# Two heads of a pair on alternate partition rows, in a fused attention and mixture-of-experts kernel

## The chip, the cores and the metric

The kernel runs on one core of a Trainium2 chip. The metric is device time in microseconds of one execution. Before the change three runs took 537.25, 535.7 and 528.64 us, so the median is 535.7 us.

## The reference, cut to what matters

The input has a batch of 8, with 8 heads, 576 positions and 64 numbers per head. Two attentions are computed and added: one over queries, keys and values that are averaged over four neighbouring positions, its output repeated four times, and one local attention in which a position sees the positions less than four away. The sum, as 4608 tokens of 512 numbers, goes through a layer of 8 experts.

```python
q_d = q.reshape(B, H, Sd, factor, D).mean(axis=3)      # the same for k, v
out_up = np.repeat(sm_attn(q_d, k_d, v_d), factor, axis=2)
mask = np.abs(pos[:, None] - pos[None, :]) < factor
scores = np.where(mask, scale * np.matmul(q, k.transpose(0, 1, 3, 2)), -1000000000.0)
x = out_up + softmax(scores) @ v                       # as 4608 rows of 512
...
do_compute = x @ w_skip > 0
e_idx = argmax(x @ w_gate, axis=1)
y[mask] = gate_w[mask, None] * (np.maximum(x[mask] @ w1[e], 0.0) @ w2[e])
out = x + y                                            # x alone where a token is skipped
```

## The kernel before, in words

The program has two parts. The attention part works through 36 tiles of 128 tokens; a tile is four groups of 32 queries, and a batch has 18 groups, so four and a half tiles. It writes its rows x to HBM and sorts the tokens to the experts on the way (`route`). The expert part then gathers each expert's rows with indirect DMAs (`load_x`), multiplies (`up_mm` L829, `down_mm` L849) and scatters the results.

**Pairs of heads.** Two heads form a pair, and there are four pairs. The queries of a pair fill 128 partitions: `Q` is [128, 4 x 576], 64 partitions for each head of a pair. The keys lie in `KB`, [128, 2, KF]: the second index is the head of the pair, and in the half of the partitions that belongs to the other head there are zeros. One product of 128 rows thus gives the scores of both heads next to each other. Before the change a pair's first head has partitions 0 to 63, its second 64 to 127 (`halves`, L162). There are two key buffers, used by batches in turn, so the zeros are written once: those of the first buffer by DVE and POOL (L635), copied by ScalarE to the second (L667), and three zero columns at each end by DVE (L642). `KD` has the same layout for the keys summed over four positions.

**V windows.** A group of 32 queries sees 38 keys, padded to KR = 48. `VB` is [96, 2, 4, 4, 64], rows of head 0 in partitions 0 to 47 and of head 1 in 48 to 95, again with zeros in the other half; `load_v` (L190) brings a tile's windows with two DMAs of 48 rows. There are three such buffers. The tile of weights `Et` is [128, 8 heads, 48], so that a pair's 96 columns, transposed, meet the 96 rows of `VB`.

**Pooled branch of a batch.** `load_q`, `load_k` (two DMAs, one for each head of the pairs; batch 0 loads in three column pieces), `load_v4`; `pool_q`, `pool_k` (L232: for each pair two sums, one per head, over four positions, on DVE, for one pair of batch 0 on POOL), `d_scores` (L243, PE), `d_max`, `d_exp`, `d_transpose`, `d_values`, `d_out`, `d_hi` and `d_lo`. Its result `up` is spread to the tiles by a product.

**One tile.** `load_v`, `scores` (L347: mask, then 32 products), `s_max` (L360), `s_sub` (L364, out of PSUM into `Et`), `s_exp` (L369), `s_sum` (L372), `add_eps`, `recip`, `norm` (L382, on POOL), `p_transpose` (L386), `p_evac`, `up_mm` (L397, needs the batch's `up`), `values` (L411), `x_out` (L418), `store_x`, then the logits for the experts.

**Order of the work.** Every step is entered in a list `nodes`, and the numbers in `ORDER` say in which order the list is carried out (L763). Each engine takes its instructions in that order, SyncE's queue with the loads and stores too: a load that waits for its buffer holds those behind it. The expert part is written out in order and has no such list.

Of the kernel before, what the change touches and what calls it, by code (L numbers as in the profile page):

```python
# [109 lines left out]
)  # L110

@with_exitstack
def tile_attention_moe(ctx, tc, qT, kT, vW, v4, vr, mask, cst, ups, cid, w9, w1, w2, out):
    nc = tc.nc
# [520 lines left out]
    for c in range(3):  # L638
        node(load_q, 0, slice(c, c + 1))
        for hh in range(2):  # L640
            node(load_k, 0, hh, slice(c, c + 1))
# [395 lines left out]
```

## Time and profile before

| what | us |
|---|---|
| runs | 528.64, 535.7, 537.25 |
| profiled execution, its own time | 527.66 |
| its span, first to last instruction | 525.5 |
| PE busy in the span | 454.1 |
| DVE busy | 317.7 |
| ScalarE busy | 248.6 |
| POOL busy | 171.7 |

The mean granted clock of PE is 0.963. A profile row for a group of instructions has line, engine, operation, output<-inputs, shapes and count, then the busy time in us and the mean ns of one, then the idle time of the engine just before them and what ended it. A table of stretches has the busy time of each engine in each stretch, the granted clock, the share of the time in which the 16 DMA engines were busy, and what they moved in GB/s. A share over 1 means packets that overlap on an engine. `hh` and the like are names of tiles in the program; SPq is SyncE's queue, which issues the loads.

### The profile page before, as it was taken

What the parts mean: (1) busy time and instruction counts of PE and PEld (TensorE: products, weight loads), DVE (VectorE), ACT (ScalarE), POOL (GpSimd) and SP (SyncE); (2) the same over time, 40 slices, a digit from 0 to 9 for tenths busy, and PEclk for the clock granted to TensorE, in tenths of its full rate; (3) what the DMA queues carried; (4) which work ended last, traced back from release to release, by engine and by line L of the source; (5) the groups of instructions that cost most, each with busy time, mean ns of one, the idle gap of its engine ahead of it and who ended that gap; (6) DMA issues with size and microseconds to landing.
All of it is one profiled execution on the core that took longest, in us unless ns stands there. A gap on an engine that the chain in (4) does not pass through costs nothing. (4 is left out here: it accounts for less than half of the span.)

```text
span 525.5 us, 13816 instructions
## 1 busy us (share of the span) xinstructions
PE 454.1 (86%) x5642; PEld 385.5 (73%) x5642; DVE 317.7 (60%) x653; ACT 248.6 (47%) x562; POOL 171.7 (33%) x184
## 2 busy tenths in 40 slices
PE   0488887986979887999649999999999999999991
PEld 0356775874857765788539998999998989898981
DVE  4988747576496675843633564555667664667521
ACT  1655764942737455755233543434454633355310
POOL 9486727064361544311060031050314040010102
PEclk9999998997999998999958999999999999999997
DMA  8999898899875797244164346553566754455201
GB/s 235 305 253 261 253 251 229 256 245 284 208 229 168 204 273 200 71 147 127 48 218 157 122 166 223 161 183 127 179 229 223 248 190 173 162 191 187 83 4 54
DMA packets 33885, 98.89 MB, mean 188 GB/s; under 512 B 5101, under 2 KB 6381, under 8 KB 33794
## 3 DMA queue, kind: packets, MB, share of 16 engines
q1 hardware_dynamic: 29954, 86.52, 56.0%
q0 software_dynamic: 3840, 11.09, 5.8%
q8 instruction: 65, 1.06, 0.9%
q14 instruction: 26, 0.21, 0.1%
HBM read 83.36 MB, written 15.73 MB: 189 GB/s over the span
## 5 line engine op out<-in xcount | busy, mean ns | idle before, releaser
L798 POOL DMA_INDIRECT out<-Y,six x24 | 24.3, 1012 | 193.3 <-DVE Y L856 190.4
L829 PE MATMUL ph<-xth,w1h 128*128 128x384 f32 (+2 forms) x256 | 82.0, 320 | 0.7 <-ACT xth L820 0.7
L829 PE MATMUL ph<-xtl,w1h 128*128 128x384 f32 (+2 forms) x256 | 80.1, 313 | 0.1
L829 PE MATMUL ph<-xth,w1l 128*128 128x384 f32 (+2 forms) x256 | 80.0, 313 | 0.0
L849 PE MATMUL py<-w2h,hh 128*128 128x512 f32 x168 | 65.8, 392 | 0.4
L849 PE MATMUL py<-w2l,hh 128*128 128x512 f32 x168 | 65.8, 391 | 0.0
L849 PE MATMUL py<-w2h,hl 128*128 128x512 f32 x168 | 65.7, 391 | 0.0
L241 DVE TENSOR_REDUCE KD<-KB 64x144 f32<-64x576 f32 x62 | 46.1, 744 | 23.5 <-DMA KB<-kT 22.8
L838 ACT ACTIVATE hh<-ph 128x384 fp32r<-128x384 f32 x64 | 31.5, 492 | 58.8 <-PE ph L829 30.7
L839 DVE SCALAR_TENSOR_TENSOR hl<-ph,hh 128x384 fp32r<-128x384 f32 x64 | 34.7, 553 | 38.3 <-ACT hh L838 38.3
L829 PEld LDWEIGHTS ph<-xth,w1h 128*128 128x128 f32 x256 | 49.4, 193 | 1.5 <-ACT xth L820 1.1
L829 PEld LDWEIGHTS ph<-xtl,w1h 128*128 128x128 f32 x256 | 49.4, 193 | 0.8 <-issue 0.4
L829 PEld LDWEIGHTS ph<-xth,w1l 128*128 128x128 f32 x256 | 49.2, 192 | 0.0
L383 POOL TENSOR_TENSOR Et<-Et,r 128x304 f32<-128x304 f32 x36 | 26.5, 740 | 60.6 <-DVE r L380 36.8
L594 DVE TENSOR_TENSOR w2l<-raw,w2h 128x1024 fp32r<-128x1024 f32 x32 | 39.0, 1220 | 10.7 <-ACT w2h L593 10.5
L609 DVE TENSOR_TENSOR w1l<-raw,w1h 128x1024 fp32r<-128x1024 f32 x32 | 39.5, 1233 | 7.3 <-ACT w1h L604 7.3
L415 PE MATMUL O<-VB,PT 96*32 96x128 f32 x1152 | 39.0, 276 | 5.3 <-ACT PT L394 3.0
L820 ACT CAST xth<-Tx 128x512 fp32r<-128x512 f32 x22 | 12.9, 588 | 63.2 <-PE Tx L817 57.3
L593 ACT CAST w2h<-raw 128x1024 fp32r<-128x1024 f32 x32 | 33.6, 1049 | 14.4 <-PE py L849 14.4
L821 DVE TENSOR_TENSOR xtl<-Tx,xth 128x512 fp32r<-128x512 f32 x22 | 15.2, 692 | 40.8 <-ACT xth L820 40.2
L357 PE MATMUL S<-KB,Q 128*32 128x76 f32 x1152 | 29.3, 244 | 11.3 <-DVE KB L623 10.5
L415 PEld LDWEIGHTS O<-VB,PT 96*32 96x32 f32 x1152 | 30.6, 110 | 11.1 <-issue 6.1
(141 smaller groups left out, 959.3 us busy)
## 6 DMA issues: line engine op xcount, KB each, us to landing
raw<-w SPq DMA_DIRECT2D x64, 512.0 KB, 4.6
VB<-vW SPq DMA_DIRECT2D x72, 192.0 KB, 5.0
out<-X SPq DMA_DIRECT2D x36, 256.0 KB, 5.1
V<-v SPq DMA_DIRECT2D x16, 512.0 KB, 7.6
KB<-kT SPq DMA_DIRECT2D x14, 576.0 KB, 10.3
Q<-qT SPq DMA_DIRECT2D x7, 1152.0 KB, 9.0
Q<-qT SPq DMA_DIRECT2D x3, 384.0 KB, 3.1
KB<-kT SPq DMA_DIRECT2D x6, 192.0 KB, 5.4
```

Source lines behind the costliest of these rows:

```text
L241: nc.vector.tensor_reduce(out=kd, in_=kv, axis=AX.X, op=ALU.add)
L357: nc.tensor.matmul(Sv[quad[j], 2 * p:2 * p + 2], lhsT=B[b]["Q"][:, o:o + QG], rhs=KBs[b % 2][:, :, k:k + KW], start=False, stop=p == 3)
L383: nc.gpsimd.tensor_tensor(out=TT[i]["E"], in0=TT[i]["E"], in1=TT[i]["r"][:, :, None].to_broadcast([128, H, KW]), op=ALU.mult)
L415: nc.tensor.matmul(O[quad[j], 128 * a:128 * a + 128], lhsT=PT[:, a, quad[j]], rhs=VB[:, :, a, j, :], start=False, stop=a == 3)
L593: nc.scalar.copy(out=hf, in_=raw)
L594: nc.vector.tensor_tensor(out=flat(lo), in0=raw, in1=hf.bitcast(F32), op=ALU.subtract)
L609: nc.vector.tensor_tensor(out=flat(lo), in0=raws[e, j], in1=flat(hi).bitcast(F32), op=ALU.subtract)
L798: ins = nc.gpsimd.indirect_dma_start(bounds_check=NOUT - 1, oob_is_err=False, **kw).ins
L829: nc.tensor.matmul(P[i][:, :n], lhsT=a[:, c, 128 * i:128 * i + 128], rhs=bb[:, c, :n], start=m == 0, stop=m == 11)
L838: nc.scalar.activation(out=hh[:, i], in_=p, func=AF.Relu)
L839: nc.vector.scalar_tensor_tensor(out=hl[:, i], in0=p, scalar=0.0, in1=hh[:, i].bitcast(F32), op0=ALU.max, op1=ALU.subtract)
L849: nc.tensor.matmul(py[k], lhsT=a[:, i, ks], rhs=bb[:, i, :], start=(j == 0 and i == 0 and m == 0), stop=(j == 3 and i == 1 and m == 2))
```

## The change

A pair's heads take turns by partition: head 0 has the even partitions, head 1 the odd ones, in queries, keys, pooled keys and V windows. The inputs are laid out for it outside the kernel. The loads of keys and V windows write every second partition, with as many rows and bytes as before. The tile of weights becomes [128, 4 pairs, 48, 2 heads]; `s_sub` writes it and `s_sum` reads it at a step of two elements, `s_exp` runs over 76 contiguous elements for each pair, and `norm` multiplies by reciprocals taken two at a time.

The first load of each key buffer (batches 0 and 1) comes from a new input `kB` that holds the zeros too, in three DMAs of 128 partitions each. The fills and copies of those zeros go, for `KB` and for `KD`. A pair's pooled key sum is one instruction over both heads and all 128 partitions; the zeros of the other head's rows are summed along, and `KD` gets its zeros from there.

`ORDER` is a new list. Counted in entries of `values` that stand ahead of them (so in tiles), the first key load, the first pooled key sum and `d_hi` of a batch stand here:

| batch | key load before, after | first pooled sum before, after | `d_hi` before, after |
|---|---|---|---|
| 2 | 0, 1 | 2, 4 | 7, 7 |
| 3 | 5, 3 | 7, 6 | 11, 13 |
| 4 | 11, 9 | 13, 13 | 18, 16 |
| 5 | 14, 13 | 17, 16 | 21, 22 |
| 6 | 21, 18 | 24, 22 | 27, 25 |
| 7 | 24, 22 | 26, 25 | 31, 30 |

Three small edits let the new order be written: `upS` and some tiles of `route` are made by whichever of their writers comes first. The diff, without the numbers of `ORDER`:

```diff
...
-def tile_attention_moe(ctx, tc, qT, kT, vW, v4, vr, mask, cst, ups, cid, w9, w1, w2, out):
+def tile_attention_moe(ctx, tc, qT, kT, kB, vW, v4, vr, mask, cst, ups, cid, w9, w1, w2, out):
...
-    Es = [kvp.tile([128, H, KR], F32, name=f"Et{i}") for i in range(3)]
+    Es = [kvp.tile([128, 4, KR, 2], F32, name=f"Et{i}") for i in range(3)]
...
-    halves = [slice(0, 64), slice(64, 128)]
+    halves = [slice(0, 128, 2), slice(1, 128, 2)]
...
+    def load_kb(b, c):
+        cols = slice((0, KO + CH, KO + 2 * CH)[c], (KO + CH, KO + 2 * CH, KF)[c])
+        nc.sync.dma_start(out=KBs[b][:, :, cols], in_=kB[b, :, :, cols])
+
...
-            rows = slice(KR * r, KR * r + KR)
-            nc.sync.dma_start(out=V[rows, r].rearrange("p a g d -> p (a g d)"), in_=vW[i, rows])
+            nc.sync.dma_start(out=V[r::2, r].rearrange("p a g d -> p (a g d)"), in_=vW[i, r])
...
-        for hh in range(2):
-            kd = KDs[b % 2][halves[hh], hh, p, :]
-            o = KO + SEQ * p
-            kv = KBs[b % 2][halves[hh], hh, o:o + SEQ].rearrange("p (i r) -> p i r", r=4)
-            if b == 0 and p == 1:
-                for r in range(3):
-                    nc.gpsimd.tensor_add(out=kd, in0=kv[:, :, 0] if r == 0 else kd, in1=kv[:, :, r + 1])
-            else:
-                nc.vector.tensor_reduce(out=kd, in_=kv, axis=AX.X, op=ALU.add)
+        kd, o = KDs[b % 2][:, :, p, :], KO + SEQ * p
+        kv = KBs[b % 2][:, :, o:o + SEQ].rearrange("p h (i r) -> p h i r", r=4)
+        if b == 0 and p == 1:
+            for r in range(3):
+                nc.gpsimd.tensor_add(out=kd, in0=kv[:, :, :, 0] if r == 0 else kd, in1=kv[:, :, :, r + 1])
+        else:
+            nc.vector.tensor_reduce(out=kd, in_=kv, axis=AX.X, op=ALU.add)
...
-        if c == 0:
+        if "upS" not in s:
...
+    heads = lambda a: a.rearrange("p (a h) -> p a h", h=2)
+
...
-        TT[i]["E"] = Es[i % 3][:, :, :KW]
-        nc.vector.tensor_tensor(out=TT[i]["E"], in0=TT[i]["S"], in1=TT[i]["nm"][:, :, None].to_broadcast([128, H, KW]),
-                                op=ALU.subtract)
+        E_ = TT[i]["E"] = Es[i % 3][:, :, :KW]
+        nc.vector.tensor_tensor(out=E_.rearrange("p a k h -> p a h k"),
+                                in0=TT[i]["S"].rearrange("p (a h) k -> p a h k", h=2),
+                                in1=heads(TT[i]["nm"])[:, :, :, None].to_broadcast([128, 4, 2, KW]), op=ALU.subtract)
...
-        nc.scalar.activation(out=TT[i]["E"], in_=TT[i]["E"], func=AF.Exp, scale=0.125)
+        E_ = TT[i]["E"].rearrange("p a k h -> p a (k h)")
+        nc.scalar.activation(out=E_, in_=E_, func=AF.Exp, scale=0.125)
...
-        nc.vector.tensor_reduce(out=r, in_=TT[i]["E"], axis=AX.X, op=ALU.add)
+        nc.vector.tensor_reduce(out=heads(r), in_=TT[i]["E"].rearrange("p a k h -> p a h k"), axis=AX.X, op=ALU.add)
...
-        nc.gpsimd.tensor_tensor(out=TT[i]["E"], in0=TT[i]["E"], in1=TT[i]["r"][:, :, None].to_broadcast([128, H, KW]),
-                                op=ALU.mult)
+        nc.gpsimd.tensor_tensor(out=TT[i]["E"], in0=TT[i]["E"],
+                                in1=heads(TT[i]["r"])[:, :, None, :].to_broadcast([128, 4, KW, 2]), op=ALU.mult)
...
-        E_ = flat(Es[i % 3])
+        E_ = Es[i % 3].rearrange("p a k h -> p (a k h)")
...
-            R[name] = smp.tile(sh, dt, name=name, bufs=2)
+            if name not in R:
+                R[name] = smp.tile(sh, dt, name=name, bufs=2)
...
-            nc.vector.scalar_tensor_tensor(out=R["eq"][:, :, :E], in0=R["df"], scalar=0.0, in1=row(C_RANK, E),
+            nc.vector.scalar_tensor_tensor(out=new("eq", [128, n, X1])[:, :, :E], in0=R["df"], scalar=0.0, in1=row(C_RANK, E),
...
-            nc.vector.tensor_tensor(out=R["oh"][:, :n], in0=R["eq"], in1=cols(R["pm"], X1), op=ALU.is_equal)
+            nc.vector.tensor_tensor(out=new("oh", [128, n + 1, X1], BF16)[:, :n], in0=R["eq"], in1=cols(R["pm"], X1), op=ALU.is_equal)
...
-            nc.vector.tensor_tensor(out=R["Bm"][:, :, 1], in0=R["ok"], in1=cols(gate, E * NBK), op=ALU.mult)
+            nc.vector.tensor_tensor(out=new("Bm", [128, n, 2, E * NBK])[:, :, 1], in0=R["ok"], in1=cols(gate, E * NBK), op=ALU.mult)
...
-    for hh in range(2):
-        node(fill, (nc.vector, nc.gpsimd)[hh], KBs[0][halves[hh], 1 - hh])
...
-        for hh in range(2):
-            node(load_k, 0, hh, slice(c, c + 1))
-    for i in range(2):
-        for o in (KO - 3, KO + 4 * SEQ):
-            node(fill, nc.vector, KBs[i][:, :, o:o + 3])
+        node(load_kb, 0, c)
...
-    for hh in range(2):
-        node(fill, nc.gpsimd, KDs[0][halves[hh], 1 - hh])
...
-    for hh in range(2):
-        node(copy, nc.scalar, KBs[1][halves[hh], 1 - hh], KBs[0][halves[hh], 1 - hh])
-        node(copy, nc.scalar, KDs[1][halves[hh], 1 - hh], KDs[0][halves[hh], 1 - hh])
...
-            for hh in range(2):
+            for c in range(3) if b == 1 else ():
+                node(load_kb, b, c)
+            for hh in range(2) if b > 1 else ():
...
-    pair = lambda a: np.ascontiguousarray(a.reshape(B, 4, 2, SEQ, HD).transpose(0, 2, 4, 1, 3)).reshape(B, 128, 4, SEQ)
+    pair = lambda a: np.ascontiguousarray(a.reshape(B, 4, 2, SEQ, HD).transpose(0, 4, 2, 1, 3)).reshape(B, 128, 4, SEQ)
...
+    kB = np.zeros((2, 128, 2, KF), f32)
+    for h in range(2):
+        kB[:, h::2, h, KO:KO + 4 * SEQ] = pair(k)[:2, h::2].reshape(2, 64, 4 * SEQ)
...
-    vW = np.ascontiguousarray(vW).reshape(NTILE, WV, 16 * HD)
+    vW = np.ascontiguousarray(vW).reshape(NTILE, 2, KR, 16 * HD)
...
-    return dict(qT=qT, kT=kT, vW=vW, v4=v4, vr=vr, mask=mask, cst=cst, ups=ups, cid=cid, w9=w9, w1=w1, w2=w2)
+    return dict(qT=qT, kT=kT, kB=kB, vW=vW, v4=v4, vr=vr, mask=mask, cst=cst, ups=ups, cid=cid, w9=w9, w1=w1, w2=w2)
```

123 rows, old and new, of the table ORDER are left out of this document.

## The prediction

> **What bounds the kernel now.** I read the page first, then a table of stretches, then the waits, then short stretches in which one kind of load moves alone. The page:
>
> ```profile
> span 525.5 us, 13816 instructions
> ...
> PE   0488887986979887999649999999999999999991
> ...
> DMA  8999898899875797244164346553566754455201
> ```
>
> From slice 20 on (262 us) PE is full and the DMA engines are half idle: that is the expert part, whose code the change does not touch. Ahead of it PE has holes, and the DMA digits read 9 in most slices up to slice 16. The table of stretches (columns: stretch, its length, then busy time and instruction count of PE, PEld, DVE, ACT, POOL, then granted clock, DMA share, GB/s) puts sizes on it:
>
> ```profile
> 0.00:15.00 15.00, 0.44 (x4) 0.17 (x4) 7.68 (x11) 2.62 (x3) 14.13 (x25) 1.00 0.88 257
> 15.00:30.00 15.00, 9.94 (x150) 6.99 (x151) 12.92 (x31) 9.82 (x22) 6.30 (x11) 1.00 1.05 284
> 30.00:250.00 220.00, 191.44 (x4007) 151.36 (x4005) 147.82 (x392) 126.81 (x376) 99.29 (x102) 0.97 0.77 214
> 250.00:273.00 23.00, 11.43 (x131) 9.15 (x129) 10.08 (x50) 6.63 (x14) 6.83 (x7) 0.76 0.39 128
> 273.00:525.00 252.00, 240.87 (x1356) 217.83 (x1356) 139.19 (x172) 102.70 (x148) 45.19 (x42) 0.97 0.49 162
> 70.00:90.00 20.00, 14.77 (x299) 11.64 (x292) 10.76 (x22) 8.07 (x16) 11.92 (x11) 0.91 0.89 239
> 110.00:130.00 20.00, 13.76 (x275) 10.61 (x274) 12.95 (x29) 5.53 (x14) 11.07 (x10) 0.88 1.03 267
> 140.00:150.00 10.00, 7.88 (x228) 6.04 (x220) 6.15 (x10) 4.95 (x10) 5.71 (x4) 1.00 1.04 256
> 180.00:210.00 30.00, 22.87 (x451) 17.92 (x449) 19.97 (x48) 16.15 (x49) 12.27 (x12) 0.95 0.90 243
> ```
>
> The attention part is the first 250 us. PE does almost nothing for 15 us, is idle 220 - 191.44 = 28.6 us between 30 and 250, and 20.7 us of that (5.2 + 6.2 + 2.1 + 7.1) lie in the last four rows, where the DMA share is 0.89 to 1.04 and the rate only 239 to 267 GB/s. The waits say what is late there (engine and line, what it waited for, total us, times, longest):
>
> ```profile
> DVE KD L241 <- DMA KB<-kT: 22.8, 6, 6.7
> POOL qd L230 <- DMA Q<-qT: 19.8, 5, 9.3
> PE S L357 <- DVE KB L623: 10.5, 1, 10.5
> ACT KB L629 <- DVE KB L623: 10.4, 1, 10.4
> PE Sd L252 <- DVE KD L241: 6.2, 3, 2.7
> ```
>
> So in six of the batches DVE stands still, 3.8 us on average, until that batch's keys land; the pooled scores on PE stand behind it. Why are full DMA engines this slow? Here are the loads as SyncE issues them, and the rate in stretches short enough to hold one kind:
>
> ```profile
> 11.94 0.97 SPq L194 DMA_DIRECT2D VB<-vW  x2
> ...
> 16.04 0.66 SPq L179 DMA_DIRECT2D KB<-kT  x1
> 17.92 0.41 SPq L176 DMA_DIRECT2D Q<-qT  x1
> 18.37 0.61 SPq L179 DMA_DIRECT2D KB<-kT  x1
> ```
>
> ```profile
> 17.00:18.00 1.00, 0.67 (x23) 0.39 (x13) 0.99 (x4) 1.00 (x1) 0.90 (x2) 1.00 0.96 201
> 20.00:22.00 2.00, 1.34 (x3) 0.37 (x2) 1.97 (x5) 1.70 (x3) 0.00 (x0) 1.00 1.03 200
> 23.00:25.00 2.00, 0.18 (x4) 0.16 (x8) 2.00 (x6) 0.91 (x5) 1.78 (x2) 1.00 1.05 404
> 26.00:27.00 1.00, 1.00 (x14) 0.50 (x2) 0.62 (x3) 0.64 (x3) 0.00 (x0) 1.00 1.03 198
> ```
>
> The queue holds VB (48 rows, twice), keys (64 rows), queries (128 rows), keys (64 rows), in this order, and the rate goes 201, 200, 404, 198. With every DMA engine counted busy, a load into 128 partitions moves at 404 GB/s and one into 64 or 48 neighbouring partitions at half of that. What bounds the attention part is therefore PE's work plus holes, and the holes are in large part half-rate loads of keys and V windows.
>
> **The change, part by part.** *Loads of keys and V windows.* A head's 64 key rows now go to every second partition of all 128, and a V window's 48 rows to every second of 96. Per batch both key loads carry 2 x 64 x 2304 x 4 B = 1.18 MB. At 200 GB/s that is 5.9 us, at 404 it is 2.9 us: 3.0 us less per batch, 18 us of DMA time for the six batches that keep this load. A tile's V window is 96 x 1024 x 4 B = 0.39 MB: 2.0 us at 201, 1.0 us at 404, so up to 36 us for 36 tiles. The trace shows no load to stepped partitions. Bounds: it stays at 200 (no gain) or reaches 404 (all of it). I take the upper end, since 128 rows run at 404 and the 48-row load (201) is no slower than the 64-row one (200): the rate does not fall with the number of rows, so where the rows lie is the likelier cause. [...]
>
> What does PE get of it? The six DVE stalls average 3.8 us; a key load that is 3.0 us shorter, with up to 1 us less for each V window queued with it, removes nearly all of a stall. The new order also loads keys earlier: counting the values() entries between a batch's first key load and its first pooled sum, batches 3 to 7 had 2, 2, 3, 3, 2 and now have 3, 4, 3, 4, 3. Behind a key load in SyncE's queue stand V windows and stores, as before. Not every hole in the four stretches ends with a key, so of their 20.7 us I take 12 (bounds: 0 if the loads stay slow, 28.6 if every hole goes).
>
> *First loads.* Batches 0 and 1 now load whole key blocks with their zeros: 128 x 2 x 2432 x 4 B = 2.49 MB each instead of 1.18. At 404 GB/s 6.2 us against 5.9 us at 200: the bytes double, the time does not. With its queries batch 0 moves 3.67 MB, 9.1 us at 404; started at about 2 us it is in at 11 to 12. Gone are the fills of the key and pooled-key zeros, the four edge fills and four ScalarE copies. Before, PE's first real scores waited 10.5 us, until about 15 us, for an edge fill (L623) that stood on DVE behind query pooling. That wait now falls to the landing of the last key piece, about 3 us earlier; and the first pooled sum needs one piece of three, (0.39 + 0.85 MB) / 404 = 3.1 us of loading, so batch 0's pooled branch starts near 8 us. I take 4 us in all (bounds: -3, if the 3.67 MB run at the 257 GB/s of the first row, 14.3 us, and +10, the whole L623 wait).
>
> *Pooled sums and element-wise steps.* The rows:
>
> ```profile
> L241 DVE TENSOR_REDUCE KD<-KB 64x144 f32<-64x576 f32 x62 | 46.1, 744 | 23.5 <-DMA KB<-kT 22.8
> ...
> L383 POOL TENSOR_TENSOR Et<-Et,r 128x304 f32<-128x304 f32 x36 | 26.5, 740 | 60.6 <-DVE r L380 36.8 <-ACT nmd L262 6.6 <-PE O L415 5.3
> ...
> L362 DVE TENSOR_REDUCE nm<-S 128x8 f32<-128x304 f32 x36 | 16.4, 466 | 9.7 <-PE S L357 9.7
> ...
> L206 DVE TENSOR_REDUCE vs<-Vr 128x64 f32<-128x256 f32 x8 | 4.8, 598 | 0.5 <-DMA Vr<-vr 0.4
> ...
> L239 POOL TENSOR_TENSOR KD<-KD,KB 64x144 f32<-64x144 f32 x4 | 2.4, 594 | 0.3
> ```
>
> One pooled sum reads 1152 elements a row instead of two reading 576. From 304 elements in 466 ns to 576 in 744 ns an element costs 1.02 ns, so the new one takes 744 + 576 x 1.02 = 1332 ns against 1488: 0.16 us for each of 31, 4.8 us of DVE. It stands at the head of a batch's pooled branch, four at a time: 0.6 us a batch. As DVE is busy only 147.8 of 220 us, I count 1 us in all (bounds 0 and 4.8).
>
> The scores tile now holds a pair's heads alternately. The subtraction (L366) writes and the sum (L374) reads at a step of 8 bytes, and the multiplication (L383) reads its reciprocals in runs of two. No row has such a step. Lower bound 0. Upper bound for DVE from L206, whose sum steps 256 bytes: 256 contiguous elements would take 466 - 48 x 1.02 = 417 ns, it takes 598, 0.71 ns more an element, so 0.21 us for 304, twice per tile. For POOL the dearest row per element is L239, 594 / 144 = 4.1 ns: 304 would take 1.25 us, 0.51 more; a tile's chain grows by at most 0.94 us. I take 0: 8 bytes lies far nearer to contiguous than 256. [...]
>
> *What else moves.* Matrix products keep their shapes and counts, and the part from 250 us on keeps its code: 0. It begins, after a pause at a clock of 0.76, with this group of products (count: shortest, median, longest ns, first and last start in us), which the sum moves forward as a whole:
>
> ```profile
> L829 PE MATMUL ph<-xth,w1h x256: 277/309/636, 273.2 to 505.8; 128*128 128x384 f32 x48, 128*128 128x256 f32 x48, 128*128 128x320 f32 x32
> ```
>
> **Sum.** 12 + 4 + 1 = 17 us. The profiled execution took 527.66 us (span 525.5), so 510.7. The runs shown have 528.64 to 537.25, median 535.7, 1.5% above it; times 535.7 / 527.66 that is **518 us**, 3.2% less.
>
> **The rivals.** *A: stepped loads stay at 200 GB/s.* For: in each key load 64 rows are still shared out, and what halves the rate could be the number of rows. Against: 48 rows run at 201, not at three quarters of 200. Then the zeros cost 2.49 MB at 404 as said, the start still gains up to 4 us, the stalls shrink only by the earlier issue, say 2 us: 527.7 - 6 = 521.7, as a median 530. [...]
>
> *B: loads double, but PE cannot use it.* PE works in order; between 30 and 250 us it is already busy 87%, so holes may reappear behind softmax chains (L390 waiting for POOL, L415 for ACT). For: only three of the holes name KD as cause, 6.2 us. Against: the four stretches with holes are those where keys land. Gain 6.2 + 1 for the start: 520.5, as a median 528.
>
> *C: slower, by the element-wise steps.* The alternating layout lengthens each tile's chain subtract, sum, multiply. Price: at the upper bounds 0.94 us a tile, 34 us for 36 tiles if every chain is on PE's path, less the 17 gained: 544.7, as a median 553. It decides from 17 / 36 = 0.47 us a tile. For: no row shows an 8-byte step or runs of two. Against: DVE has 72 us and POOL 121 us idle between 30 and 250 us to cover it, and the bound comes from a step 32 times as long.
>
> **How the numbers follow.** Forecast 0.58, A 0.17, B 0.15, C 0.10. A measurement of this kernel can tell about 2% from no change, 10.7 us: faster means under 525, slower over 546.4. Of the forecast's 0.58 some 0.52 lie under 525; A and B add 0.08; C gives slower 0.09. Faster 0.60, same 0.31, slower 0.09. The range: below, every hole of 28.6 us gone with 1 for DVE, 498.1, as a median 506; with a little of the start I go to 504. Above it reaches past A and B to 536, leaving out C.
>
> **What would show it.** Right: stretches with key loads alone at 350 GB/s or more; the wait of DVE L241 on KB under 8 us; PE's first scores by 13 us; the expert part's first L829 near 256 us instead of 273; L241 at 1.33 us, 31 of them at most. Wrong: key stretches still near 200 (A); fast loads but PE idle between 30 and 250 us still over 20 us (B); L366 and L374 longer by 0.2 us or L383 over 1 us (C).

## The result, and the profile after

The changed kernel takes 505.8 us (median of 4 runs, 505.33 to 508.53) against 532.17 for the kernel before in the same comparison (4 runs, 524.71 to 537.25). The ratio is 0.961, with a 95% interval of 0.953 to 0.970. Run again later beside other kernels, the changed kernel had 504.1 against 532.69, 0.951 (0.945 to 0.957). The forecast was 3.2% less (518 of 535.7); 3.9% and 4.9% were measured, and 505.8 lies near the lower end of the range of 504 to 536. The profiled execution took 505.92 us, 21.7 less than the 527.66 of before.

From the page after, the same lines as before:

```profile
span 504.1 us, 13771 instructions
...
PE   0678899989997999998499999999999999999991
...
DMA  7986996989899663451554555464666753555201
```

The attention part now ends within slice 18. The table of stretches of the kernel after, with the same columns as before (stretch, length, busy time and count for PE, PEld, DVE, ACT, POOL, clock, DMA share, GB/s):

```profile
0.00:15.00 15.00, 0.00 (x0) 0.00 (x0) 2.21 (x2) 1.28 (x1) 8.94 (x19) 1.00 0.82 291
15.00:30.00 15.00, 10.12 (x131) 5.94 (x131) 13.79 (x27) 7.20 (x29) 5.06 (x7) 1.00 0.91 297
30.00:235.00 205.00, 188.48 (x4115) 151.75 (x4114) 154.22 (x385) 127.45 (x372) 101.88 (x104) 0.99 0.74 241
235.00:253.00 18.00, 8.66 (x42) 7.17 (x42) 6.91 (x36) 4.63 (x10) 7.10 (x7) 0.54 0.43 136
253.00:504.00 251.00, 239.96 (x1356) 216.94 (x1356) 139.16 (x172) 102.23 (x147) 44.79 (x42) 0.98 0.48 162
```

Between 30 us and the end of the attention part PE is idle for 205 - 188.5 = 16.5 us, where it was 28.6 before. (Counted to the last tile's output in each kernel, so that both stretches end alike, it is 28.6 and 15.3.) The DMA engines are a little less busy (0.74 against 0.77) while they move more in a second (241 against 214 GB/s). In the first 15 us PE now does nothing at all. The waits of the kernel after:

```profile
PE Sd L252 <- DVE KD L241: 16.6, 1, 16.6
...
DVE KD L241 <- DMA KB<-kB: 11.5, 1, 11.5
...
POOL qd L232 <- DMA Q<-qT: 2.7, 1, 2.7
...
DVE KD L241 <- DMA KB<-kT: 2.1, 1, 2.1
```

The waits of the pooled sums for the keys of batches 2 to 7 have shrunk from 22.8 us in six to 2.1 us in one; the wait of the pooled queries from 19.8 to 2.7. New is one wait of 11.5 us for `kB`, the first keys with their zeros, and behind it PE's first product at 16.6 us. And this is how the loads run after the change; SyncE's queue, then two stretches that it fills, then one with V windows alone (issued at 180.49):

```profile
43.53 0.68 SPq L178 DMA_DIRECT2D KB<-kT  x1
44.30 0.55 SPq L175 DMA_DIRECT2D Q<-qT  x1
44.90 0.65 SPq L178 DMA_DIRECT2D KB<-kT  x1
```

```profile
46.00:50.00 4.00, 3.53 (x94) 2.48 (x82) 3.90 (x14) 3.85 (x16) 1.90 (x4) 1.00 1.01 410
```

```profile
182.00:183.00 1.00, 1.00 (x56) 1.00 (x52) 1.00 (x2) 0.11 (x1) 1.00 (x1) 1.00 0.98 238
```

Once they run, keys, queries, keys move through at 410 GB/s from the first to the last (the microsecond ahead of it comes up at the end), so a load of 64 stepped rows runs as fast as one of 128. (Four microseconds at 410 GB/s are 1.64 MB of the three loads' 2.36; the next two read 409 and 399.) V windows, 48 stepped rows, run at 238, only a fifth faster than the 201 of before.

Where the 21.4 us of the span come from, by two groups of instructions (count, durations, first and last start): the tiles' outputs, before and after, and the first expert product.

```profile
L420 ACT COPY X<-O x36: 567/586/617, 47.4 to 252.6; 128x512 f32<-128x512 f32 x36
```

```profile
L424 ACT COPY X<-O x36: 581/586/601, 39.5 to 230.7; 128x512 f32<-128x512 f32 x36
```

```profile
L825 PE MATMUL ph<-xth,w1h x256: 277/309/637, 252.9 to 484.6; 128*128 128x384 f32 x48, 128*128 128x256 f32 x48, 128*128 128x320 f32 x32
```

Before, the first tile's output came at 47.4 us and the last at 252.6. The first is 7.9 us earlier; the 36 tiles take 191.2 us from first to last instead of 205.2, 14.0 less; from the last tile to the first expert product it is 22.2 instead of 20.6, 1.6 more. That makes 20.3, and the expert part gives 1.1.

Waiting is not all of the 20.3. Here is everything up to the first expert product, before and then after:

```profile
0.00:273.20 273.20, 213.25 (x4286) 167.67 (x4286) 178.50 (x481) 146.09 (x416) 126.75 (x143) 0.95 0.76 213
```

```profile
0.00:252.90 252.90, 207.21 (x4286) 164.80 (x4286) 177.05 (x445) 140.47 (x412) 122.88 (x137) 0.96 0.74 240
```

With 4286 products in each, PE is idle 14.3 us less (60.0 to 45.7) and busy 6.0 us less: the same products took less time. Cut into stretches of 10 us between 30 and 230 us, the granted clock is below 0.9 in four before (0.83 from 80 us, 0.76 and 0.89 from 120, 0.86 from 200) and in one after (0.83 from 60).

### The profile page after: what moved, and what is told of

It reads as the page before. It is cut to its first block, busy times and chain, and to the rows that moved or that the text cites. A ratio compares the mean times of both kernels' runs of the same rounds, so it can differ in the third digit from the quotient of the medians.

```text
span 504.1 us, 13771 instructions
## 1 busy us (share of the span) xinstructions
PE 447.2 (89%) x5642; PEld 381.8 (76%) x5642; DVE 316.3 (63%) x617; ACT 242.8 (48%) x558; POOL 167.8 (33%) x178
## 5 line engine op out<-in xcount | busy, mean ns | idle before, releaser
L241 DVE TENSOR_REDUCE KD<-KB 128x288 f32<-128x1152 f32 x31 | 40.8, 1339 | 13.7 <-DMA KB<-kB 11.5
L252 PE MATMUL Sd<-KD,qd 128*128 128x288 f32 x64 | 23.9, 470 | 19.2 <-DVE KD L241 16.6
L817 DVE TENSOR_TENSOR xtl<-Tx,xth 128x512 fp32r<-128x512 f32 x22 | 15.2, 692 | 40.5 <-ACT xth L816 37.2
L794 POOL DMA_INDIRECT xr<-out,gix x24 | 27.7, 1154 | 30.9 <-DMA raw<-w 23.8
```

What stands on the lines that cost most here:

```text
L241: nc.vector.tensor_reduce(out=kd, in_=kv, axis=AX.X, op=ALU.add)
L252: nc.tensor.matmul(pairs(S), lhsT=B[b]["qd"][:, n, :128], rhs=kd[:, :, n, :], start=True, stop=True)
L794: ins = nc.gpsimd.indirect_dma_start(bounds_check=NOUT - 1, oob_is_err=False, **kw).ins
```

## The experiments

Each kernel was timed beside the kernel before on one chip; its median there was 532.5 in the first group of four, 533.8 in the second, 532.7 in the third. Numbers in brackets are 95% intervals of the ratio to it.

**All rows back in blocks.** The change with queries, keys, V windows and weights laid out as before; order, first loads and merged sums stay.

```diff
-    halves = [slice(0, 128, 2), slice(1, 128, 2)]
+    halves = [slice(0, 64), slice(64, 128)]
...
-            nc.sync.dma_start(out=V[r::2, r].rearrange("p a g d -> p (a g d)"), in_=vW[i, r])
+            nc.sync.dma_start(out=V[KR * r:KR * r + KR, r].rearrange("p a g d -> p (a g d)"), in_=vW[i, r])
```

> The changed kernel with every head's rows back in one block (queries, keys, key zeros, V windows and the tile of weights as before the change), but with the new order, the new first loads and one pooled sum a pair. Placement theory (loads to neighbouring partitions run at half rate, and that held PE up): key stretches fall back to about 200 GB/s, PE's idle time between 30 us and the end of the attention part grows from 16 us to 25 us or more, and the time is 514 to 524 us against 506. Order theory (the new issue order and the earlier key loads brought the gain): the rate falls too, but the loads stand early enough, and the time stays at 505 to 510 us.

Measured: 522.7 us, 0.985 (0.977 to 0.993). Its keys, queries, keys, in stretches of its own trace, and its wait for keys:

```profile
45.00:46.00 1.00, 0.52 (x6) 0.30 (x2) 1.00 (x4) 1.00 (x6) 0.64 (x2) 1.00 1.04 200
47.00:49.00 2.00, 2.00 (x80) 1.70 (x76) 1.79 (x8) 2.00 (x11) 1.05 (x2) 1.00 1.04 406
50.00:51.00 1.00, 1.00 (x6) 0.68 (x6) 0.90 (x4) 1.00 (x4) 0.00 (x0) 1.00 1.12 221
```

```profile
DVE KD L241 <- DMA KB<-kT: 14.7, 4, 7.1
```

With nothing but the rows moved, the rate falls to half and the waits for keys come back, 14.7 us of them. The time goes up by 17 us by the medians, 13 to 18 by the ratios. Of the 17.2 us between the two profiled spans, 8.4 are idle time of PE and 8.8 are products that take longer (PE is busy 456.0 us instead of 447.2, at a mean clock of 0.953 instead of 0.968). The placement theory holds: the order alone does not give the gain.

**Only queries and keys in blocks.** The first and the layout part of the diff above, V windows stay alternate.

> The changed kernel with queries and keys in blocks again, V windows and weights left alternating. Placement theory, keys first: 512 to 520 us, most of what all blocks together cost, and DVE waits for keys again, over 10 us in all. If instead the V windows carry the gain of placement: at most 509 us. Order theory: 505 to 510 us.

Measured: 520.1 us, 0.978 (0.966 to 0.990); waits for keys 12.3 us. By the medians 14 of the 17 us that blocks cost come with queries and keys; the intervals of the two kernels overlap.

**Only V windows and weights in blocks.**

> The changed kernel with V windows and the tile of weights in blocks again (element-wise steps contiguous as before), queries and keys left alternating. The trace after the change shows V windows alone at 238 to 250 GB/s, against 200 before, so keys-first placement expects little: 506 to 510 us, V stretches at about 200 GB/s. If the V windows carry the gain: 512 us or more. If the alternating element-wise steps cost anything, this kernel is faster than 505 us.

Measured: 509.5 us, 0.959 (0.951 to 0.967). As expected for a V rate that rises by a fifth: by the ratios between 1 us less and 4 us more than the changed kernel (0.961 and 0.951 in two comparisons), and 2.6 us between the medians of the two kernels above; the intervals overlap, so the size is not settled, but it is small. Nor do contiguous element-wise steps make it faster.

**The old order with the new layout.** Every step at its old place in the list.

> The changed kernel with the old issue order: each step at its old place, the removed fills and copies left out, the new first key loads at the place of the old ones. Placement theory: keys land sooner at their old places too, so 512 to 522 us, over half of the way from 532 to 506. Order theory: 525 us or more, since the old order was laid out around late keys and the new one brings the gain.

Measured: 508.0 us, 0.957 (0.948 to 0.965). Better than the placement theory's own guess of 512 to 522: almost the whole gain is there without the new order. Its first tile's output comes at 46.3 us, against 39.5 in the changed kernel, and its last at 233.1 against 230.7:

```profile
L420 ACT COPY X<-O x36: 566/585/605, 46.3 to 233.1; 128x512 f32<-128x512 f32 x36
```

So the new order starts the tiles 6.8 us sooner, and 4.4 us of that are given back before the last one.

**The first loads alone.** The kernel before in blocks and in its old order, with `kB` for batches 0 and 1 and without the fills and copies; its two pooled sums a pair run over all 128 partitions, as the zeros now come with the keys.

> The kernel before (blocks, old order, two pooled sums a pair, here over all partitions) with the new first loads alone: keys of batches 0 and 1 come with their zeros, fills and copies are gone. The prediction gave the start 4 us: 526 to 530 us against 532. If the start brings no gain, since the doubled bytes eat it: 531 to 536. If all of the 10 us between the kernel before and the changed kernel in blocks come from here: 520 to 524.

Measured: 531.4 us (12 runs), 0.996 (0.992 to 0.9997). About 2 us (0.2 to 4 by the interval), of the 4 forecast.

**The first loads and the keys' rows.** The kernel just above, with queries and keys on alternate partitions and their inputs laid out for it, nothing else.

```diff
-    halves = [slice(0, 64), slice(64, 128)]
+    halves = [slice(0, 128, 2), slice(1, 128, 2)]
```

> The kernel before in its old order, with V windows in blocks and two pooled sums a pair, the new first loads, and queries and keys on alternate partitions: against the run with the first loads alone (531.4 us) only the rows of queries and keys differ. If the keys' rate is the cause of most of the gain, with no help of the new order: 511 to 517 us, DVE's wait for keys under 10 us instead of 24.6. If the order has to go with it: 522 us or more.

Measured: 509.2 us, 0.959 (0.953 to 0.964). The wait for keys, with the first loads alone and here:

```profile
DVE KD L239 <- DMA KB<-kT: 24.6, 6, 6.7
```

```profile
DVE KD L239 <- DMA KB<-kT: 6.7, 5, 2.1
```

Between this and the kernel just above lie the rows of queries and keys alone: the ratio goes from 0.996 to 0.959, some 20 us (each beside the kernel before, on two chips). This is most of the gain of the change, in the old order too. POOL's wait for the queries, which stand behind a key load in the queue, is shorter too, 8.8 us against 29.0 there and 19.8 in the kernel before. The clock differs along with the waits: the mean granted clock of an execution, as the median of a kernel's runs, is 0.948 to 0.953 where the key rows lie in blocks (the kernel before, the first loads alone, and the two that put key rows back) and 0.957 to 0.970 in the kernels with alternate key rows. A hole thus seems to cost more than its own length, but no run changes the clock alone, so that it is the holes that lower it is not shown.

**Two pooled sums a pair.**

```diff
-        kd, o = KDs[b % 2][:, :, p, :], KO + SEQ * p
+        o = KO + SEQ * p
+        for h in (slice(0, 1), slice(1, 2)):
+            kd = KDs[b % 2][:, h, p, :]
```

> The changed kernel with two pooled key sums a pair again, one for each head, each over all 128 partitions (rows of the other head give the zeros). By the prediction's step the merged sum saves 0.15 us for each of 31, mostly under other work: 506 to 509 us. If the merged sum carries a real part of the gain: 511 us or more. If it costs, because in batch 0 one sum over both heads waits for all three pieces of the keys: under 505 us.

Measured: 509.6 us, 0.957 (0.952 to 0.961). The changed kernel itself had 0.951 (0.945 to 0.957) and 0.961 (0.953 to 0.970), so by the ratios the merged sum brings anything from 3 us lost to 3 us gained; the 1 us forecast cannot be told from nothing.

**Two sums in batch 0 alone.**

> The changed kernel with two pooled key sums a pair in batch 0 alone. After the change the first sum waited until 15.1 us, though its piece of the keys had landed at 8.75 us. Theory: a sum over both heads spans columns of all three pieces and is held until the last lands; split, the first sum starts at 9 to 11 us, PE's first product at 10 to 13 us instead of 16.6, and the time falls by 1 to 4 us (502 to 505). Rival: the piece itself, or the queries, are late, and the start stays at 15 us and the time at 505 to 508 us. A third: the start moves but PE spends it waiting later, time unchanged.

Measured: 510.1 us, 0.957 (0.952 to 0.962): no gain. The trace, in order of time (start, duration, engine and line, what it waited for):

```profile
9.25 0.75 DVE L243 TENSOR_REDUCE KD<-KB 128x144 f32<-128x576 f32 x1 [5.70 <-DMA KB<-kB]
...
15.36 0.75 DVE L243 TENSOR_REDUCE KD<-KB 128x144 f32<-128x576 f32 x1 [5.35 <-DMA KB<-kB]
...
16.26 1.30 PE L254 MATMUL Sd<-KD,qd 128*128 128x288 f32 x2 [16.26 <-DVE KD L243]
```

The first head's sum starts at 9.25 us; the second head's, on columns that came in the same piece, only at 15.36, and the product needs both. A piece of `kB` is one load over both heads, so between its first and its last column lie columns of other pieces, and the program's wait covers all of them.

**V windows as 64 rows.** 16 rows of zeros are loaded along, into all 128 partitions; the products read 96 rows as before.

```diff
-    VBs = [kvp.tile([WV, 2, 4, 4, HD], F32, name=f"VB{i}") for i in range(3)]
+    VBs = [kvp.tile([128, 2, 4, 4, HD], F32, name=f"VB{i}") for i in range(3)]
...
+    vW = np.pad(vW, ((0, 0), (0, 0), (0, 64 - KR), (0, 0)))
```

> The changed kernel with V windows loaded as 64 rows (the 48, and 16 rows of zeros that no product reads) into every second one of 128 partitions, a third more bytes. V windows alone moved at 238 to 250 GB/s after the change, keys at about 400. Theory: 48 rows, three for each DMA engine, lie unevenly, and 64 stepped rows run like the keys: V stretches at 350 GB/s or more, time 503 to 506 us. Rival: a V load is slow for its size (0.2 MB) or its 4 KB rows: still near 250 GB/s, so more bytes at the same rate, 507 to 511 us.

Measured: 504.0 us, 0.948 (0.943 to 0.953). A stretch with V windows alone (issued at 185.18, with nothing ahead of them in the queue):

```profile
187.00:188.00 1.00, 1.00 (x10) 0.92 (x8) 0.14 (x1) 0.82 (x2) 0.00 (x0) 1.00 0.97 381
```

A third more bytes in less time: 0.52 MB at 381 GB/s are 1.38 us, 0.39 MB at 238 are 1.65. Size and row length are not what held them back.

**The changed kernel, 64 rows, and one load for each head, side by side.** The last one splits the load of each piece in batch 0, besides the sum, and has the 64 rows.

```diff
+        for h in (slice(0, 1), slice(1, 2)) if b == 0 else (slice(0, 2),):
-        nc.sync.dma_start(out=KBs[b][:, :, cols], in_=kB[b, :, :, cols])
+            nc.sync.dma_start(out=KBs[b][:, h, cols], in_=kB[b, :, h, cols])
```

> The changed kernel itself once more, for comparison on the same chip: 505 to 508 us.

Measured: 504.1 us (502.20 to 507.63), 0.951 (0.945 to 0.957).

> The changed kernel with V windows loaded as 64 rows, once more beside the changed kernel on one chip: 499 to 505 us, 2 to 5 us less than the changed kernel beside it. If the first look was luck of that chip: within 1 us of it.

Measured: 502.6 us (500.35 to 504.89), 0.946 (0.940 to 0.951). 1.5 us below the changed kernel beside it, with overlapping runs: less than expected, and not settled.

> V windows as 64 rows, and in batch 0 one key load and one pooled sum for each head and piece (six loads instead of three). With the sums split alone the first head's sum began at 9.25 us and the second's only at 15.36, when the last piece had landed. Theory: a load over both heads holds every column between its first and last, the other head's too; with a load for each head both sums start by 10 us and PE's first product by 12 us instead of 16; the time falls by 1 to 4 us against 64 rows alone. Rival: PE starts earlier and waits later (the rest of batch 0 still lands at 15 us): no more than 1 us.

Measured: 499.4 us (497.82 to 500.33), 0.940 (0.935 to 0.945), all six runs below the changed kernel's lowest. It is the fastest version found, 4.7 us under the changed kernel. Its start:

```profile
5.70 0.75 DVE L244 TENSOR_REDUCE KD<-KB 128x144 f32<-128x576 f32 x1 [2.13 <-DMA KB<-kB]
...
7.94 0.75 DVE L244 TENSOR_REDUCE KD<-KB 128x144 f32<-128x576 f32 x1 [1.49 <-DMA KB<-kB]
...
9.87 1.33 PE L255 MATMUL Sd<-KD,qd 128*128 128x288 f32 x2 [9.87 <-POOL qd L225]
```

The first head's sum starts at 5.70 us, the second's at 7.94, and PE's first product at 9.87. It now waits for the pooled queries, no longer for keys. Against 64 rows alone that is 3.2 us, with no overlap of the runs, and about half of the 7.0 us by which PE starts earlier (16.9 there).

## Why the prediction was right, and where it was not

*Key loads, 12 us of the 17.* Right in cause, and too small. The rate went from 200 to 410 GB/s, and PE's idle time between 30 us and the last tile's output fell by 13.3 us (28.6 to 15.3), close to the 12. But with only the rows of keys and queries changed about 20 us of the time go. That the position of rows and not their number halves the rate was argued from one row of the trace; the blocks run, with the same 64 rows at 200 beside the queries' 406, shows it. Why neighbouring rows halve it, no run shows. Rival A is out: two loads of 64 rows each ran at 410 GB/s, each spread over all partitions.

*Matrix products, no gain forecast.* Up to the first expert product PE was busy 6.0 us less with the same products, as worked out above. It is the term that the sum lacked; that it goes with the clock is likely, and not shown.

*From the profile to the median.* The sum gave 510.7 us for the profiled execution and 505.92 was measured, 4.8 less. The factor 1.015 then added 7.3 us that the changed kernel does not have: its profiled execution stands at its median, while that of the kernel before stood 4.5 us below its own. Together this is the 12 us between 518 and 505.8.

*The new order's earlier key loads.* Counted as part of the cause, and it is hardly needed: with the old order 508.0 us. In blocks the same order, with the first loads (0.4% by themselves) and merged sums, brings 1.5%: it helps where loads are slow. Early issue and a fast load take away the same waits, which would be why the two gains do not add.

*V windows, "up to 36 us" of DMA time at 404.* Mis-sized. They reached 238, not 404, so 0.3 us a tile instead of 1, 11 us of DMA time. The prediction took all stepped loads as one kind; the bound should have been put between 201 and 404. It cost little, for V windows held up little.

*The start, 4 us.* The step that failed. The forecast had the first pooled sum begin near 8 us, after one piece; it began at 15.10, after all three, because a sum or a load over both heads is held by columns of the other pieces (split by head, the sums began at 9.25 and 15.36 us, and with the loads split too at 5.70 and 7.94). PE's first product on keys came at 16.6 us, where before it came at 15.2, and in the first 30 us PE is idle no less than before (19.9 us and 19.6). Two signs of the forecast are missed here: first scores by 13 us, and under 8 us of waits of DVE L241 on `KB` (13.7, of which 11.5 are at the start). The loads also ran at 226 GB/s from 2 to 5 us, with the DMA engines 0.77 busy, and not at 404 at once:

```profile
2.00:5.00 3.00, 0.00 (x0) 0.00 (x0) 1.56 (x2) 0.04 (x1) 3.00 (x4) 1.00 0.77 226
5.00:8.00 3.00, 0.00 (x0) 0.00 (x0) 0.00 (x0) 0.00 (x0) 3.00 (x7) 1.00 0.91 292
8.00:15.00 7.00, 0.00 (x0) 0.00 (x0) 0.00 (x0) 0.00 (x0) 1.56 (x5) 1.00 1.02 398
```

The first loads brought about 2 us by themselves. The tiles' first output is 7.9 us earlier all the same; with the old order it is 1.1 us earlier, so this is the new order's doing. It puts batch 0's pooled branch ahead of the tiles' scores: the pooled products (L252) start at 16.6 us and the tiles' (L357) at 20.4, where before it was 19.1 and 15.2, and the first `upH`, which the tiles' outputs need, is made at 35.0 us instead of 42.4 (41.3 in the old order).

*Pooled sums and element-wise steps.* The rows after:

```profile
L241 DVE TENSOR_REDUCE KD<-KB 128x288 f32<-128x1152 f32 x31 | 40.8, 1339 | 13.7 <-DMA KB<-kB 11.5 <-DMA KB<-kT 2.1
L387 POOL TENSOR_TENSOR Et<-Et,r 128x304 f32<-128x304 f32 x36 | 25.9, 725 | 62.7 <-DVE r L384 36.6 <-DVE rd L324 6.5 <-PE O L419 4.8
...
L368 DVE TENSOR_TENSOR Et<-S,nm 128x304 f32<-128x304 f32 x36 | 16.7, 467 | 4.9 <-PE T L394 4.3
...
L378 DVE TENSOR_REDUCE r<-Et 128x8 f32<-128x304 f32 x36 | 16.5, 462 | 8.6 <-ACT Et L374 8.3
```

1339 ns for the merged sum, 1332 forecast. The subtraction takes 467 ns (470 before), the sum 462 (458), the multiplication 725 (740): runs of two on POOL and a step of 8 bytes on DVE cost nothing here, and rival C is out.

*Rival B*, that PE cannot use faster loads, did not come about: PE's idle time fell with the waits. What is left of it, 16.5 us, no longer stands behind keys: DVE waits for those of batches 2 to 7 for 2.1 us in all. What ends the rest was not taken apart.

## What to carry to other kernels

Look at the rate of each kind of load alone, in stretches where the DMA engines read as fully busy: here a load at half of another's rate (200 beside 404 GB/s) had its fault in where its rows lie, and spreading 64 rows over all partitions cured it (410 GB/s) without a byte less. In this program a load or an instruction that spans two regions of a tile is held by everything between them (the first pooled sum began at 15.10 us, and at 5.70 with loads and sums split by head), so pieces that are to be used early want loads and sums of their own. Issuing earlier and loading faster removed the same wait here (508.0 us with the old order, 505.8 with the new): count their gains once. And count the products behind a removed wait too: here they ran 6 us shorter.

## What the runs showed of the hardware that was not expected

Stepped rows are not all alike: 64 of them into every second partition run at 410 GB/s, 48 into every second one of 96 at 238, and padding the 48 to 64 brings 381. Why 48 are slow was not tried further; shared out evenly they would be three for each of the 16 DMA engines, and they reach into 96 partitions only, and either could be it. The microsecond ahead of the stretch of keys, queries, keys in the changed kernel runs far slower, at 80 GB/s with the DMA engines counted as 0.94 busy, before 410 sets in. It follows a microsecond in which they stood nearly idle (0.03 busy); the runs leave the cause open:

```profile
45.00:46.00 1.00, 1.00 (x33) 0.83 (x36) 1.00 (x3) 0.33 (x1) 0.00 (x0) 1.00 0.94 80
```
